# Sparse attention feeding an MLP mixer: the global sums moved into the next period, three transposes put into PV's PSUM slot, scores spaced by two dense tiles

## The chip, the cores and the metric

The kernel runs on one core of a Trainium2 chip. Its engines are named here as the profile names them: PE (TensorE, matrix products), DVE (VectorE), ACT (ScalarE), POOL (GpSimd) and SP (SyncE, which only issues transfers). The metric is the device time of one execution in microseconds, as the median of repeated runs.

## The reference

The kernel computes a sparse attention followed by a token and channel mixer.

```python
# q, k, v: [8, 8, 576, 64] (batch, head, token, dim); 8 global tokens
scores = q @ k.T / sqrt(64)
mask = |i - j| <= 32  or  i is global  or  j is global
x = softmax(scores where mask else -1e9) @ v      # -> [8, 576, 512], heads side by side
h = relu(x.T @ w_tok1) @ w_tok2                   # tokens 576 -> 256 -> 576
u = x + h.T
out = u + relu(u @ w_ch1) @ w_ch2                 # channels 512 -> 1536 -> 512
```

The inputs and the output are float32; the kernel computes in float16 and sums in float32.

## The kernel before

**Batches and tiles.** The eight batches go through the kernel one behind the other. The 576 tokens of a batch are four tiles of 128 and one of 64. Heads go in four pairs, p = 0 to 3. The last 64 tokens of two batches share one tile in the channel mixer, which is therefore done in the odd batches.

**The steps of a batch**, with their functions (lines in the listing below and in the profile):

- casts (L383, L386): the loaded q and k go to float16, mostly on ACT. `casts(b)` is a list of ten, c(0) to c(4) are its pairs: the last 64 tokens, then head pairs 0 to 3.
- `TR` (L427) transposes the last 64 tokens on PE; `TRE` (L438) copies the result out on DVE.
- `T(b, p)` (L400) transposes q and k of a head pair on PE, eight 128x128 transposes into one PSUM tile pT; `TE` copies it out on DVE, q at L406 and k at L412. `t` is both.
- `globals_` (L392) puts the global tokens' queries beside the others.
- `S_(b, p, part)` (L458): banded scores, in two parts, each followed by its exponential on ACT (L470). `s2` is both parts. `SM` (L476 `eg`, L481 `e_all`) masks them on DVE and picks out `eg`, the weights of the global rows.
- `GK` (L515 to L517): scores of the global keys; exponential on ACT (L527, L528), mask on DVE (L532).
- `v_odd` (L373, L374): a copy of v shifted by 64 tokens, two DVE copies.
- `OG` (L539): the global rows' sums over all tokens, twenty small matmuls that read `eg` of all four head pairs; DVE spreads the result into `rf` (L544).
- `PV(b, tau)` (L656, L665): the attention's output for one token tile, from `rf`, the masked exponentials and v. DVE divides by the row sums (L678, L679) and writes x.
- `M1(b, ch)` (L692): token mixer in, one token tile at a time; after the last one ACT takes the ReLU (L700; in batch 1 ACT and DVE take half each, L697 and L698) and writes `a1`.
- `M2(b, part)` (L716): token mixer out, in three parts; DVE adds x and writes `u` (L721, the last part L724). `M3` (L733, L736) turns u into `uT` with transposing DMAs on SP's queue; in batch 1 `M3p` does it on PE (L745, L747).
- `M4(b, j)` (L755): channel mixer in, twelve tiles of four 128x512 matmuls, each followed by a ReLU on ACT (L758). `M4l` is the same for the shared last tile.
- `M5(b, tau, part)` (L781): channel mixer out, two parts of six 128x512 matmuls for each token tile; DVE adds u (L785, the last tile L788) and writes `osb`, which SP stores.

M4, M4l and M5 are the *dense tiles*. All the rest is the sparse work.

**Periods.** Period b interleaves the dense tiles of batch b with the sparse work of later batches: `n = b + 1` is finished (PV, M1, M2, M3), and `m = b + 2` is begun (T, S, GK). The order is written out by hand. In the lists below `D` (None) stands for "the next dense tile"; `play` takes the list from left to right, and puts dense tiles that are left over at its end. Period 0 has its own list (`period_0`). Period 1 is merged by weights (`sparse2`, `merge`); in it T(3,1) and T(3,2) come out next to each other. Periods 2 to 7 play `first_half` with the twelve M4 (and three M4l in odd periods) and `second_half` with the eight or ten M5. Period 6 has nothing of batch m, and period 7 is dense tiles alone. Batch 0's sparse work is done ahead of period 0, in another order.

Every engine works its instructions in the order in which the lists emit them. So a step's place in a list sets its place in the queues of PE, DVE, ACT and SP alike.

**PSUM.** Three pools share the eight banks. psS (`pss`) has two slots of two banks, psV (`psv`) one slot of two banks, psM (`psm`) two slots of one bank. The slots of a pool are used in turn, and a tile waits until the slot's last tile has been read. psM holds the results of M4, M4l and M5 (and T and TR of batches 0 and 2). psS holds S, M1, M2 and the odd PV. psV holds GK, OG and the even PV, in batches other than 2. T and TR take a slot by the expressions in their first lines, which the change edits. In the kernel before, T(m, p) of batches from 3 on lies in psS for even p and in psV for odd p.

**Loads.** SP loads q and k of the batch after next once the casts of the batch before have read the buffers, ahead of the transposing DMAs of M3 in its queue. POOL loads v once PV has read the old one.

Of the kernel before, what the change touches and what calls it, by code (L numbers as in the profile page):

```python
# [9 lines left out]
F16 = mybir.dt.float16  # L10
# [5 lines left out]
P = 128  # L16
NT = 5
# [27 lines left out]
def kernel(  # L45
# [13 lines left out]
    B, H, S, D = q.shape  # L59
# [4 lines left out]
    NP = H // 2  # L64
# [306 lines left out]
    def v_odd(b, hs=slice(0, H), eng=nc.vector):  # L371
        i = b % 2
        eng.tensor_copy(out=vod[i][HQ:P, :, hs], in_=vsh[i][HQ:P, 0 : NT - 1, hs])  # L373
        eng.tensor_copy(out=vod[i][0:HQ, :, hs], in_=vsh[i][0:HQ, 1:NT, hs])  # L374
# [16 lines left out]
    def globals_(b):  # L391
        nc.vector.tensor_copy(  # L392
            out=qTs[b % 2][:, :, :, 0:NG], in_=gT[:, b].unsqueeze(2).to_broadcast([P, NP, NT, NG])
        )

    def T(b, p):
        pT = (psm if b in (0, 2) else psv if b == 1 or p % 2 else pss)([P, 2, 512], F16, name=f"pT_{b}_{p}")
        for ti, n in enumerate((qn, kn)):
            for i in range(4):
                nc.tensor.transpose(  # L400
                    out=pT[:, ti, P * i : P * i + P], in_=n[b % 2][:, i, 2 * p : 2 * p + 2, :], identity=ident
                )
        st[b]["pT", p] = pT
# [15 lines left out]
        TEk(b, p)  # L419

    def TR(b):
        pr = (psm if b in (0, 2) else psv)([P, 2, 4, NP * 16], name=f"pr_{b}")
        sel = ident.rearrange("p (n r x) -> p r n x", n=NP, r=2)
        for ti, n in enumerate((qr, kr)):
            for i in range(4):
                for par in range(2):
                    nc.tensor.matmul(  # L427
                        pr[64 * par : 64 * par + 64, ti, i, :], lhsT=n[b % 2][:, i, :], rhs=sel[:, par], start=True, stop=True
                    )
        st[b]["pr"] = pr  # L430
        if b > 0:
            TRE(b)
# [39 lines left out]
    def SM(b, p):  # L472
        e2 = e_all[:, 2 * p : 2 * p + 2]
        if b > 0:
            gc = bass.AP(tensor=e2.tensor, offset=e2.offset, ap=[e2.ap[0], [QS, NT], [ES, 2], [1, NG]])
            nc.vector.tensor_tensor(  # L476
                out=eg[:, :, 2 * p : 2 * p + 2, 0:NG], in0=gc, in1=egm.unsqueeze(2).to_broadcast([P, NT, 2, NG]), op=ALU.mult
            )
        bm = bandm.rearrange("p c x -> p (c x)")[:, 0:ES]
        for par in range(2):  # L480
            nc.vector.tensor_mul(out=e2[:, par], in0=e2[:, par], in1=bm)  # L481
# [26 lines left out]
    def GK(b):  # L508
        s = st[b]
        ps = (psv if b != 2 else pss)([P, 2, 512], name=f"gk_{b}")  # L510
        for p in range(NP):
            o = ps[32 * p : 32 * p + 32]
            qv = qTs[b % 2][:, p, :, NG:QS]
            w = kgz[:, b, p, :]
            nc.tensor.matmul(o[:, 0, 0:384], lhsT=w, rhs=qv[:, 0:3], start=True, stop=True)  # L515
            nc.tensor.matmul(o[:, 1, 0:128], lhsT=w, rhs=qv[:, 3], start=True, stop=True)
            nc.tensor.matmul(o[:, 1, 128:192], lhsT=w, rhs=qv[:, 4, 0:LAST], start=True, stop=True)  # L517
        s["gk"] = ps
        if b > 0:
            LX(b)  # L520
            LM(b)
# [8 lines left out]
    def LM(b):  # L530
        lf = st[b]["lf"]
        nc.vector.tensor_mul(out=lf, in0=lf, in1=mf)  # L532

    def OG(b):
        s = st[b]
        ps = (psv if b != 2 else pss)([P, 2, VW], name=f"og_{b}")
        for c in range(NT):
            for p in range(NP):
                nc.tensor.matmul(  # L539
                    ps[32 * p : 32 * p + 32], lhsT=eg[:, c, 2 * p : 2 * p + 2, :],  # L540
                    rhs=vsh[b % 2][:, c, 2 * p : 2 * p + 2, :], start=(c == 0), stop=(c == NT - 1),
                )
        rf = mb.tile([P, NP, 2, VW], F16, tag="rf", name=f"rf_{b}")
        nc.vector.tensor_tensor(  # L544
            out=rf, in0=ps.unsqueeze(1).to_broadcast([P, NP, 2, VW]),
            in1=blk.rearrange("p (n r) -> p n r", r=2).unsqueeze(3).to_broadcast([P, NP, 2, VW]), op=ALU.mult,
        )
        s["rf"] = rf
# [135 lines left out]
    def M1(b, ch):  # L684
        s = st[b]
        if ch == 0:
            ps = pss([P, 2, 512], name=f"a1p_{b}")
            s["a1p"], s["a1pp"] = [ps[:, 0], ps[:, 1]], ps
        ps = s["a1p"]
        for tt in range(2):  # L690
            w = w1[:, ch, P * tt : P * tt + P] if ch < NT - 1 else w1l[:, b % 2, P * tt : P * tt + P]
            nc.tensor.matmul(ps[tt], lhsT=w, rhs=x16s[b % 2][:, ch, :], start=(ch == 0), stop=(ch == NT - 1))  # L692
        if ch < NT - 1:
            return
        a1 = mb.tile([P, 2, DM], F16, tag="a1", bufs=1, name=f"a1_{b}")
        if b == 1:
            nc.scalar.activation(out=a1[:, 0], in_=s["a1pp"][:, 0], func=AF.Relu)  # L697
            nc.vector.tensor_scalar(out=a1[:, 1], in0=s["a1pp"][:, 1], scalar1=0.0, scalar2=None, op0=ALU.max)  # L698
        else:
            nc.scalar.activation(out=a1, in_=s["a1pp"], func=AF.Relu)  # L700
        s["a1"] = a1
        s["u16"] = mb.tile([P, 4, DM], F16, tag="u16", name=f"u16_{b}")
        if b % 2 == 0:
            s["ul"] = mb.tile([P, DM], F16, tag="ul", name=f"ul_{b}")
        else:
            s["ul"] = st[b - 1]["ul"]
# [85 lines left out]
    def t(b, p):  # L792
        T(b, p)
        TE(b, p)
# [37 lines left out]
    def s2(b, p):  # L832
        return lambda: (S_(b, p, 0), S_(b, p, 1))

    def period_0():
        n, m = 1, 2
        D = None
        c2 = casts(m)
        c1 = [lambda ti=ti, p=p: cast_qk(1, ti, p, nc.scalar.copy) for p in (2, 3) for ti in range(2)]
        u = [D, D, D, D, D, D, lambda: TR(n), lambda: globals_(n), D, lambda: t(n, 0), *c1[:2], D]  # L840
        u += [lambda: t(n, 1), *c1[2:], lambda: (load_qk1(2), load_v16(2)), D, s2(n, 0), D, lambda: t(n, 2), lambda: SM(n, 0), D, s2(n, 1), D]
        u += [lambda: t(n, 3), lambda: SM(n, 1), s2(n, 2), lambda: v_odd(n), D, lambda: SM(n, 2), lambda: GK(n), s2(n, 3), D]
        u += [lambda: SM(n, 3), lambda: OG(n), D, lambda: PV(n, 0), lambda: PV(n, 1), D, lambda: PV(n, 2), lambda: PV(n, 3), D]
        u += [*c2, lambda: PV(n, 4), lambda: [M1(n, ch) for ch in range(NT - 1)], D, lambda: M1(n, NT - 1), lambda: globals_(m), D]
        u += [lambda: M2(n, 0), lambda: M2(n, 1), lambda: TR(m), D, lambda: M3p(n, 0), lambda: t(m, 0)]
        u += [lambda: M3p(n, 1), lambda: (M2(n, 2), M3(n, 2)), lambda: t(m, 1)]
        u += [s2(m, 0), lambda: t(m, 2), lambda: SM(m, 0)]
        return u

        return u  # L850

    def first_half(b):
        n, m = b + 1, b + 2
        D = None
        cs = casts(m) if m < B else []

        def c(k):
            return cs[2 * k : 2 * k + 2]

        def tt(p):  # L860
            return [lambda: t(m, p)] if m < B else []

        def pv(tau):
            return lambda: PV(n, tau)

        if n == B:
            return []
        u = [D, *([lambda: OG(n)] if b == 2 else []), D, pv(0), pv(1), *c(0), D, *c(1), D, pv(2), pv(3), *c(2), D, lambda: [M1(n, ch) for ch in range(3)], D]
        if b == 2:
            u += [lambda: gather_t(1)]  # L870
        u += [pv(4), *c(3), D, lambda: M1(n, 3), D, *([lambda: TR(m)] if m < B else []), lambda: M1(n, 4), *c(4)]
        if m < B:
            u += [lambda: load_v16(m), lambda: globals_(m)]
        if m + 1 < B:
            u += [lambda: (load_rest(m + 1), load_qk(m + 1, slice(0, H)))]
        u += [D, *tt(0), D, lambda: (M2(n, 0), M3(n, 0)), D, *tt(1), lambda: (M2(n, 1), M3(n, 1)), D, *tt(2)]
        u += [lambda: (M2(n, 2), M3(n, 2) if n % 2 else None), D]
        return u

    def second_half(b):  # L880
        m = b + 2
        D = None
        if m >= B:
            return []
        return [D, s2(m, 0), D, lambda: t(m, 3), lambda: SM(m, 0), D, s2(m, 1), D, lambda: SM(m, 1), D, s2(m, 2), D,
                lambda: SM(m, 2), lambda: GK(m), lambda: v_odd(m), s2(m, 3), D, lambda: SM(m, 3), D, lambda: OG(m)]

    def dense(b):
        u = [(0.86, lambda j=j: M4(b, j)) for j in range(NJ)]
# [188 lines left out]
```

## Time and profile before

| | |
|---|---|
| median of 14 runs | 335.9 us (333.7 to 339.18) |
| profiled execution | 339.65 us, of which the profile's span is 337.6 us |
| PE busy | 317.0 us, 94% of the span |
| DVE, ACT, POOL busy | 192.2, 155.4, 62.2 us |
| M4 and M5 on PE (L755, L781) | 94.9 and 102.3 us busy |
| mean granted PE clock | 0.977 |
| period 2 / 3 / 4 / 5 / 6 begins (its first M4) | 128.39 / 164.93 / 204.54 / 238.71 / 278.31 us |

The span runs from the first to the last instruction; the execution's own time has some 2 us around it. A PE instruction's shown length includes the time until its result has left the array, while the next one starts before that; therefore the distance from start to start tells what a group of matmuls costs. A row of the timeline has start, length, engine, line, operation, output and inputs, shape, count, and in brackets the idle time before it with what ended it. A row of a windows answer gives for a stretch of time the busy time of PE, PE's weight loads, DVE, ACT and POOL, then the granted PE clock as a share of full speed, and the DMA load. In the page's second part the granted PE clock stands in tenths for 40 equal slices of the span.

### The profile page before, as it was taken

The page shows a single profiled execution, that of the slowest core. Times are in us where ns is not written, and L with a number is a line of the kernel's source. Part 1 is how long each engine was busy: PE and PEld are TensorE (multiplying, and loading weights), DVE is VectorE, ACT ScalarE, POOL GpSimd, SP SyncE. Part 2 cuts the span into 40 slices and gives each one's busy share as a digit, 9 for nine tenths or more (in the row PEclk, how much of TensorE's full clock was granted, in tenths as well). Part 3 has the DMA queues.
Part 4 walks back from the last instruction along what each step waited for, and adds up shares of the span by engine and source line. Part 5 has one row for each costly group of instructions (what it writes and reads, how often), then busy time and mean ns, then how long its engine had stood idle before and what let it go on. Part 6 is the DMA issues. An engine that isn't in the chain of part 4 may idle for free.

```text
span 337.6 us, 8236 instructions
## 1 busy us (share of the span) xinstructions
PE 317.0 (94%) x3505; PEld 175.8 (52%) x3505; DVE 192.2 (57%) x414; ACT 155.4 (46%) x281; POOL 62.2 (18%) x95
## 2 busy tenths in 40 slices
PE   4988999798899999999999999999999999999994
PEld 4757845355446544454455645444556445444641
DVE  7385557658952777485737475477737564231021
ACT  3460378702848045654475444744474333503600
POOL 5696569130021001300030002200000000000000
PEclk9996799799999999999999999999999999999998
DMA  7999997991877952969196714995102121051013
GB/s 207 210 145 222 279 182 225 172 111 54 202 124 76 264 163 58 90 207 184 65 93 192 161 65 90 75 265 133 58 0 49 49 94 33 2 140 62 2 63 92
DMA packets 78198, 41.85 MB, mean 124 GB/s; under 512 B 54482, under 2 KB 72274, under 8 KB 78162
## 3 DMA queue, kind: packets, MB, share of 16 engines
q0 software_dynamic: 38608, 12.88, 31.6%
q1 hardware_dynamic: 39552, 28.45, 31.5%
q8 instruction: 27, 0.44, 0.6%
q14 instruction: 9, 0.07, 0.1%
q10 hardware_dynamic: 2, 0.00, 0.0%
HBM read 36.11 MB, written 9.44 MB: 135 GB/s over the span
## 4 chain that ended last, share of the span: by engine, by line
PE 78%; DVE 16%; issue 3%; ACT 2%; DVEq 0%; ACTq 0%
PE op L781 24%; PE b1p L755 21%; PE a1p L692 5%; PE hp L716 4%; PE pv L656 3%; PE b1lp L768 3%; PE pT L400 3%; PE pv L665 3%; PE s L458 3%; DVE e_all L481 2%; DVE kT L412 2%; DVE vod L373 1%; DVE vod L374 1%; DVE qT L406 1%; PE warm L208 1%
## 5 line engine op out<-in xcount | busy, mean ns | idle before, releaser
L755 PE MATMUL b1p<-uT,wc 128*128 128x512 f16 x384 | 94.9, 380 | 0.8 <-ACT b L758 0.6
L758 ACT ACTIVATE b<-b1p 128x512 f16<-128x512 f32 x96 | 57.0, 598 | 76.8 <-PE b1p L755 76.8
L781 PE MATMUL op<-wc,b 128*128 128x512 f16 x384 | 91.1, 383 | 0.0
L470 ACT ACTIVATE e_all<-s 128x544 f16<-128x544 f32 (+1 forms) x64 | 40.9, 685 | 38.4 <-issue 26.0
L781 PEld LDWEIGHTS <-b 128*128 128x128 f16 x384 | 35.4, 98 | 39.5 <-issue 0.8
L755 PEld LDWEIGHTS <-wc 128*128 128x128 f16 x384 | 35.0, 98 | 39.8 <-issue 2.2
L361 POOL DMA_DIRECT2D vsh<-in_v_dram x35 | 29.5, 849 | 140.5 <-DVE rr L678 125.6
L785 DVE TENSOR_TENSOR osb<-u,op 128x512 f32<-128x512 f16 x32 | 22.0, 686 | 53.2 <-PE op L781 51.0
L678 DVE RECIPROCAL rr<-pv 128x8 f32<-128x8 f32 (+1 forms) x35 | 7.1, 204 | 32.4 <-PE pv L665 32.4
L481 DVE TENSOR_TENSOR e_all<-e_all,bandm 128x616 f16<-128x616 f16 x56 | 24.3, 476 | 1.0
L679 DVE TENSOR_TENSOR x<-pv,rr 128x512 f16<-128x512 f32 (+1 forms) x35 | 24.2, 691 | 1.2
L406 DVE COPY qT<-pT 128x512 f16<-128x512 f16 x30 | 20.6, 686 | 7.2 <-PE pT L400 6.8
L721 DVE TENSOR_TENSOR u<-x,hp 128x1024 f16<-128x1024 f16 x14 | 17.0, 1218 | 12.1 <-PE hp L716 12.1
L412 DVE COPY kT<-pT 128x512 f16<-128x512 f16 x30 | 20.4, 682 | 1.9 <-PE pT L400 1.3
L716 PE MATMUL hp<-a,w 128*128 128x512 f16 x72 | 19.1, 379 | 1.3 <-DVE u L721 1.3
L656 PE MATMUL pv<-rf,lf 128*64 128x264 f16 x126 | 18.7, 288 | 0.9 <-DVE kgz L355 0.7
L665 PEld LDWEIGHTS <-e_all 128*64 128x64 f16 x504 | 18.3, 112 | 0.2
L665 PE MATMUL pv<-vsh,e_all 128*64 128x66 f16 x280 | 18.4, 196 | 0.0
L386 ACT CAST qn<-lq 128x512 f16<-128x512 f32 x27 | 16.6, 614 | 3.5 <-DMA lq<-in_q_dram 3.5
L386 ACT CAST kn<-lk 128x512 f16<-128x512 f32 x27 | 16.8, 621 | 1.5 <-DMA lk<-in_k_dram 1.5
L458 PE MATMUL s<-qT,kT 64*64 64x136 f16 (+2 forms) x704 | 16.3, 216 | 1.2 <-DVE ul L724 0.7
L458 PEld LDWEIGHTS <-kT 64*64 64x64 f16 x704 | 10.8, 107 | 12.6 <-issue 10.9
(175 smaller groups left out, 366.1 us busy)
## 6 DMA issues: line engine op xcount, KB each, us to landing
out_dram<-osb SPq DMA_DIRECT2D x32, 256.0 KB
lq<-in_q_dram SPq DMA_DIRECT2D x5, 1024.0 KB
lk<-in_k_dram SPq DMA_DIRECT2D x5, 1024.0 KB
wc<-in_moe_w_ch_dram POOLq DMA_DIRECT2D x6, 512.0 KB
vsh<-in_v_dram POOLq DMA_DIRECT2D x21, 128.0 KB
lq<-in_q_dram POOLq DMA_DIRECT2D x2, 1024.0 KB
lk<-in_k_dram POOLq DMA_DIRECT2D x2, 1024.0 KB
vsh<-in_v_dram POOLq DMA_DIRECT2D x14, 96.0 KB
```

The costliest lines, as they stand in the source:

```text
L361: nc.gpsimd.dma_start(out=vsh[b % 2][r0:r1, c, :, 0:D], in_=v[b, :, j0 : j0 + (r1 - r0), :].rearrange("h p d -> p h d"),)
L386: eng(out=(qn, kn)[ti][b % 2][:, :, hs].rearrange("p i h d -> p h i d"), in_=(lq, lk)[ti][:, hs])
L412: eng(out=kTs[b % 2][:, p, WIN : WIN + 512].rearrange("p (x i) -> p x i", i=4), in_=st[b]["pT", p][:, 1].rearrange("p (i x) -> p x i", i=4),)
L458: nc.tensor.matmul(ps[o, par, i0 - a : i1 - a], lhsT=kT[r, HQ * j : HQ * j + HQ], rhs=qf[r, i0:i1], start=b > 0, stop=b > 0 or j in js[-2:],)
L470: nc.scalar.activation(out=e2[:, :, a:z], in_=ps[:, :, 0 : z - a], func=AF.Exp, scale=scale)
L481: nc.vector.tensor_mul(out=e2[:, par], in0=e2[:, par], in1=bm)
L656: nc.tensor.matmul(ps[r0 : r0 + 64, hf, 0 : NP * VW], lhsT=s["lf"][:, HQ * t : HQ * t + HQ], rhs=s["rf"][:, 2 * hf : 2 * hf + 2], start=Tr ...
L665: nc.tensor.matmul(ps[r0 : r0 + 64, hf, VW * hh : VW * hh + VW], lhsT=e_all[:, h, lo : lo + HQ], rhs=(vod if t % 2 else vsh)[b % 2][:, tau ...
L716: nc.tensor.matmul(ps[:, i, :], lhsT=w2[:, ch, P * tau - sh : P * tau - sh + P], rhs=s["a1"][:, ch, :], start=(ch == 0), stop=(ch == 1),)
L755: nc.tensor.matmul(ps, lhsT=wc1[:, cc, P * j : P * j + P], rhs=s["uT"][:, cc, :], start=(cc == 0), stop=(cc == 3))
L758: nc.scalar.activation(out=s["b1"][:, j, :], in_=ps, func=AF.Relu)
L781: nc.tensor.matmul(ps, lhsT=w, rhs=wc2[:, j, :], start=(j == 0), stop=(j == NJ - 1))
```

## The change

Nothing is added or removed; slots and orders change.

- T(m, p) of batches from 3 on: p = 1, 2 and 3 all take psV; only p = 0 takes psS. TR of batch 1 takes psS instead of psV.
- Period 0: v_odd stands behind S(1,3) and a dense tile; OG stands one dense tile later; the dense tile between M1(1,4) and M2(1,0) is gone from there (it is the one ahead of OG).
- Periods 2 to 6, `first_half`: OG(n) stands behind the period's first dense tile and ahead of two more, then PV. Before, it stood at the end of the last period (in period 2, as now, behind the first dense tile). The casts c(0) to c(4) come earlier. No dense tile is left between M1(n,4) and T(m,0). T(m,2) stands behind M2's second part and a dense tile, and T(m,3) behind M2's third part, where before it was in the second half.
- Periods 2 to 5, `second_half`: T(m,3) and OG(m) are gone. S(m,1) stands two dense tiles behind S(m,0), S(m,2) two behind S(m,1); v_odd comes one dense tile earlier.

```diff
     def T(b, p):
-        pT = (psm if b in (0, 2) else psv if b == 1 or p % 2 else pss)([P, 2, 512], F16, name=f"pT_{b}_{p}")
+        pT = (psm if b in (0, 2) else psv if b == 1 or p > 0 else pss)([P, 2, 512], F16, name=f"pT_{b}_{p}")
     def TR(b):
-        pr = (psm if b in (0, 2) else psv)([P, 2, 4, NP * 16], name=f"pr_{b}")
+        pr = (psm if b in (0, 2) else pss if b == 1 else psv)([P, 2, 4, NP * 16], name=f"pr_{b}")
     def period_0():
-        u += [lambda: t(n, 3), lambda: SM(n, 1), s2(n, 2), lambda: v_odd(n), D, lambda: SM(n, 2), lambda: GK(n), s2(n, 3), D]
-        u += [lambda: SM(n, 3), lambda: OG(n), D, lambda: PV(n, 0), lambda: PV(n, 1), D, lambda: PV(n, 2), lambda: PV(n, 3), D]
-        u += [*c2, lambda: PV(n, 4), lambda: [M1(n, ch) for ch in range(NT - 1)], D, lambda: M1(n, NT - 1), lambda: globals_(m), D]
+        u += [lambda: t(n, 3), lambda: SM(n, 1), s2(n, 2), D, lambda: SM(n, 2), lambda: GK(n), s2(n, 3), D]
+        u += [lambda: v_odd(n), lambda: SM(n, 3), D, lambda: OG(n), D, lambda: PV(n, 0), lambda: PV(n, 1), D, lambda: PV(n, 2), lambda: PV(n, 3), D]
+        u += [*c2, lambda: PV(n, 4), lambda: [M1(n, ch) for ch in range(NT - 1)], D, lambda: M1(n, NT - 1), lambda: globals_(m)]
         u += [lambda: M2(n, 0), lambda: M2(n, 1), lambda: TR(m), D, lambda: M3p(n, 0), lambda: t(m, 0)]
     def first_half(b):
-        u = [D, *([lambda: OG(n)] if b == 2 else []), D, pv(0), pv(1), *c(0), D, *c(1), D, pv(2), pv(3), *c(2), D, lambda: [M1(n, ch) for ch in range(3)], D]
+        u = [D, lambda: OG(n), *c(0), D, D, pv(0), pv(1), *c(1), D, *c(2), D, pv(2), pv(3), D, lambda: [M1(n, ch) for ch in range(3)], *c(3), D]
         if b == 2:
             u += [lambda: gather_t(1)]
-        u += [pv(4), *c(3), D, lambda: M1(n, 3), D, *([lambda: TR(m)] if m < B else []), lambda: M1(n, 4), *c(4)]
+        u += [pv(4), D, lambda: M1(n, 3), *c(4), D, *([lambda: TR(m)] if m < B else []), lambda: M1(n, 4)]
         ...
-        u += [D, *tt(0), D, lambda: (M2(n, 0), M3(n, 0)), D, *tt(1), lambda: (M2(n, 1), M3(n, 1)), D, *tt(2)]
-        u += [lambda: (M2(n, 2), M3(n, 2) if n % 2 else None), D]
+        u += [*tt(0), D, lambda: (M2(n, 0), M3(n, 0)), *tt(1), D, lambda: (M2(n, 1), M3(n, 1)), *tt(2), D]
+        u += [lambda: (M2(n, 2), M3(n, 2) if n % 2 else None), *tt(3)]
     def second_half(b):
-        return [D, s2(m, 0), D, lambda: t(m, 3), lambda: SM(m, 0), D, s2(m, 1), D, lambda: SM(m, 1), D, s2(m, 2), D,
-                lambda: SM(m, 2), lambda: GK(m), lambda: v_odd(m), s2(m, 3), D, lambda: SM(m, 3), D, lambda: OG(m)]
+        return [D, s2(m, 0), D, D, lambda: SM(m, 0), s2(m, 1), D, lambda: SM(m, 1), D, s2(m, 2), lambda: v_odd(m), D, lambda: SM(m, 2),
+                lambda: GK(m), s2(m, 3), D, lambda: SM(m, 3), D]
```

## The prediction

> **What bounds the kernel now.** I read the shares and the clock row, then the chain of work, then TensorE's and VectorE's timelines of one period at a time.
>
> ```profile
> PE 317.0 (94%) x3505; PEld 175.8 (52%) x3505; DVE 192.2 (57%) x414; ACT 155.4 (46%) x281; POOL 62.2 (18%) x95
> ...
> PEclk9996799799999999999999999999999999999998
> ...
> PE 78%; DVE 16%; issue 3%; ACT 2%; DVEq 0%; ACTq 0%
> ```
>
> TensorE is busy nearly throughout and owns the chain; VectorE's 16% are the places where TensorE stands still for it. The change adds no work, so I only ask where these stops are, which go and which come. TensorE, period 3:
>
> ```profile
> 183.01 1.03 PE L755 MATMUL b1p<-uT,wc 128*128 128x512 f16 x4
> 183.87 0.39 PE L400 MATMUL pT<-ident,qn 128*128 128x128 f16 x4
> 184.09 0.39 PE L400 MATMUL pT<-ident,kn 128*128 128x128 f16 x4
> 184.81 0.59 PE L716 MATMUL hp<-a,w 128*128 128x512 f16 x2 [0.33 <-DVE u L721]
> ...
> 201.20 0.80 PE L539 MATMUL og<-vsh,eg 128*32 128x132 f16 x20
> ```
>
> From start to start an unhindered T takes 0.45 us (181.70 to 182.14); this one takes 0.94: 0.49 lost, since M2 waits for a psS slot. OG runs from 201.20 to the next start at 201.94, 0.74; unhindered it needs 0.42 (62.02 to 62.41 for its last seventeen matmuls): 0.32 lost to `eg`. At the end of even periods the first two M4 take 2.06 (164.93 to 166.99) instead of 1.83: 0.23 lost to an `osb` that frees a psM slot. VectorE beside it:
>
> ```profile
> 182.34 0.69 DVE L406 COPY qT<-pT 128x512 f16<-128x512 f16 x1
> 182.95 0.68 DVE L412 COPY kT<-pT 128x512 f16<-128x512 f16 x1
> 183.55 1.21 DVE L721 TENSOR_TENSOR u<-x,hp 128x1024 f16<-128x1024 f16 x1
> 184.68 0.68 DVE L406 COPY qT<-pT 128x512 f16<-128x512 f16 x1
> ```
>
> So a pair of TE copies holds VectorE 1.20 us, one `u` 1.13; a copy's result is there 0.68 after its start, and TensorE goes on 0.06 later (`u` ends at 184.76, M2 starts at 184.81). A copy starts 0.20 after its matmuls' end. Period 1, TensorE, then VectorE:
>
> ```profile
> 116.61 0.39 PE L400 MATMUL pT<-ident,qn 128*128 128x128 f16 x4
> ...
> 117.06 0.39 PE L400 MATMUL pT<-ident,qn 128*128 128x128 f16 x4
> ...
> 117.51 1.46 PE L781 MATMUL op<-wc,b 128*128 128x512 f16 x6
> 118.86 0.38 PE L400 MATMUL pT<-ident,qn 128*128 128x128 f16 x4
> ```
>
> ```profile
> 116.84 0.68 DVE L785 TENSOR_TENSOR osb<-u,op 128x512 f32<-128x512 f16 x1
> 117.43 0.68 DVE L406 COPY qT<-pT 128x512 f16<-128x512 f16 x1
> 118.03 0.68 DVE L412 COPY kT<-pT 128x512 f16<-128x512 f16 x1
> ```
>
> T(3,1) and T(3,2) run back to back because they lie in different slots; the first is evacuated only at 118.71. Last, period 0's OG, and the windows over what follows it:
>
> ```profile
> 59.97 0.30 PE L539 MATMUL og<-vsh,eg 128*32 128x132 f16 x3
> 62.02 0.46 PE L539 MATMUL og<-vsh,eg 128*32 128x132 f16 x17 [1.75 <-DVE eg L476]
> 62.41 2.58 PE L781 MATMUL op<-wc,b 128*128 128x512 f16 x6
> ```
>
> ```profile
> 62.60:66.00 3.40, 3.40 (x28) 1.59 (x28) 0.89 (x2) 3.20 (x7) 0.00 (x0) 0.50 1.83 163
> ```
>
> OG stands 2.0 us, and then the clock is at half rate for 3.4 us: six M5 take 2.51 and PV 1.58 where they take 1.40 and 1.08 elsewhere, 1.6 us more.
>
> **What the Trainium skill says.** "PSUM — Partial Sum Buffer", PSUM bank collisions raise a hardware error, has every reuse of a bank guarded by a semaphore: a one-slot pool makes each new T wait for the last one's evacuation; the 0.49 above is such a wait. "TensorE: Matmul & The Clock Gate", Part 1, says ScalarE and VectorE are strict FIFO and matmuls keep program order, so a T that waits holds up all behind it; the trace agrees (M2 at 184.81 waits in place). The same part gives a free-running activity window of 3413 ns after which a lightly used array falls to half rate; the trace shows one such stretch from 62.6 to 66.0 after the 2.0 us stop. As the window is free-running, that loss need not come in every execution.
>
> **The change part by part**, t = 0 at M1(n,4)'s end, in us.
>
> *First half, periods 2 to 5.* Now M1, T0, dense, M2(0), T1, dense, M2(1), T2, dense, M2(2), T3. `a1` (L700, 1.02) starts 0.26 after M1 (143.47 to 143.73), so M2(0) may go at 1.34; T0 (0.45) and a dense tile (0.86) reach 1.31: 0.03 to 0.10 lost, I take 0.07 (the casts c(4) now stand ahead of it on ScalarE, two of 0.50, but end about 0.6 before M1 does; without that cover up to 1.0). M2(0) 1.38 to 2.24; `u` 2.44 to 3.57. T1 at 2.24 finds psV free. Dense, M2(1) to 4.42. T2 would start at 4.42, but TE(1) waits behind `u`: 3.57 to 4.77, result at 4.17+0.68 = 4.85; T2 at 4.91, **0.49 lost**. The next `u` 4.77 to 5.90. T2, dense, M2(2) end at 6.65; TE(2) 5.90 to 7.10, result at 7.18; T3 at 7.24, **0.59 lost**. Old stop here 0.49. Net +0.66 a period, four periods: **+2.6**.
>
> *Period 1* changes only through T's slots: T(3,2) goes from psS to psV. T2 may start at 118.77 instead of 117.06: 1.71 lost; TE(2) runs 119.41 to 120.6, result at 120.69; T3 follows the M5 at 120.5 and waits to 120.75. T3 was at 118.86: **+1.9**. Nothing after it has slack of its own: exponentials, `eg` and OG all hang on TensorE.
>
> *Second half.* T3 is gone from it. SM and v_odd keep their order; v_odd's two copies (0.73 each) go ahead of the third `osb`. `eg`(3) is written 1.7 us before OG, which stands behind one more M4; the last `osb` frees its slot 0.5 before the second M4. Without these covers the old 0.32 and 0.23 come back. Gain 0.32 at the ends of periods 2 to 5, 0.23 at 2 and 4: **-1.7**. Period 2's PV no longer waits for `rf` (M4 1.13 instead of 0.97): **-0.2**.
>
> *Period 6* has no T between M1(7,4) and M2(7,0): one dense tile (0.86) against `a1` ready at 1.34 (290.54 to 290.80, + 1.02 + 0.06): **+0.5**.
>
> *Period 0.* TR(1) in psS spares T(1,0) the wait for TR's copies: -0.28. S(1,3) then ends at 58.29, two dense tiles at 60.98, and OG starts. VectorE: `osb` 59.79 to 60.40 (its M5 ends at 59.59), v_odd to 61.86, `eg` to 62.05: OG stops for 1.05 instead of 2.0 and ends at 62.48. From there to M1(1,4)'s end, at full clock, 1.40 + 1.08 + 1.40 + 1.08 + 1.40 + 0.60 + 1.74 + 1.30 + 0.43 = 10.43 in both orders (M5, PV, M5, PV, M5, PV, M1, M5, M1): 72.91 now, 72.84 before with its OG ending at 62.41. But the dense tile put ahead of OG is missing behind M1(1,4), where it covered `a1` (74.70 to 76.03); TensorE now stands about 1.5 there, and M2(1,0) ends as long after M1(1,4) as before (2.3). So the tile moved from one stop to another: **0.0**. The stop of 1.05 leaves two thirds of a window busy, so the half-rate stretch should go: **-1.6 where it was**. T(1,p) and T(2,p) keep their slots.
>
> *Queues.* SP's loads of the next q and k wait for c(4) and are issued some 2 us earlier, ahead of the transposing DMAs as before; `uT` is due 15 us after its `u`. POOL's loads of v wait for PV, 0.9 later, and are read 30 us on. Both are hidden; a late `uT` would stop M4 by its full lateness.
>
> Sum: 2.6 + 1.9 - 1.7 - 0.2 + 0.5 = +3.1. The profiled execution (339.65, span 337.6, 2.05 around it) had the half-rate stretch: 339.65 + 3.1 - 1.6 = 341.1. It lies 3.75 above the median 335.9 and at the top of the runs shown (333.7 to 339.18), which stand in three groups about 2 us apart, as if such stretches came in some and not in others. So for the median I count half of the 1.6: 335.9 + 3.1 - 0.8 = **338.2**.
>
> **The rivals.** *The clock pays in full* (18%): the median run had the stretch; 335.9 + 3.1 - 1.6 = 337.4. For: 59.2 to 62.6 is idle by more than half. Against: the lower half of the runs. *A new half-rate stretch* (15%): period 1's stop of 1.7 leaves about half of a window busy; the stop at 60 us left less than half. 338.2 + 1.6 = 339.8. *Half the waits* (12%): TE comes sooner than its queue lets me think, all nine new waits are half as long, -3.1: 335.1. *Faster* (5%): T2 and T3 find psV free, because the copies do not queue behind `u` and `osb`; 1.9 + 4 x 1.08 = 6.2 less, 332.0. It decides for faster once the nine waits sum to under 2.2. Against: thirty copies of 0.68 with hardly a spread, in a fixed order. That the edits do nothing is excluded, as the slots and orders differ in every period.
>
> **How the numbers follow.** Forecast 50%, its own range 337.2 to 339.2. 0.5% (1.7 us: below 334.2, above 337.6) is about what can be told from no change. Above 337.6 lie nine tenths of the forecast, the new stretch and a little of the full clock gain: 0.64; faster 0.05; the rest 0.31. The range 336.4 to 340.3 leaves out the two fast cases and the tail of the slow one; the unknown wake-up (0.06 to 0.13 in nine places) moves it by 0.6 at most.
>
> **What would show it.** TensorE: in periods 2 to 5 a stop of about 0.5 before T2 and 0.6 before T3, released by L412; one of 1.7 before T(3,2) in period 1; OG without a stop from period 3 on; about 1.05 before OG and 1.5 in M2 in period 0; 0.5 before M2(7,0). In the clock row no half rate near 62 us. Wrong if the T stops are missing, if half rate shows near 118 us, or if period 0's end moves by more than the clock.

## The result and the profile after

The changed kernel takes 339.8 us (median of 10 runs, 337.97 to 341.27); beside it the kernel before took 334.76 us (47 runs). The ratio is 1.0139, 95% interval 1.0109 to 1.0169: about 4.7 us slower. The forecast was 338.2 us in a range of 336.4 to 340.3, slower.

Executions of one kernel differ by several us with their mean granted PE clock; "at full clock" below means the median over the executions whose mean clock was 0.995 or more. At full clock the kernel before takes 334.5 us (53 of the 106 executions that ran beside the experiments below) and the changed one 338.25 (6 of 12): +3.8 us. The other half of the changed kernel's executions lies at clocks of 0.984 to 0.991, mostly near 340.7, which is why its median over all is higher.

The page of the profiled execution after (337.49 us, span 335.4): busy shares, clock row, and the chain's shares.

```profile
PE 309.4 (92%) x3505; PEld 168.7 (50%) x3505; DVE 193.5 (58%) x414; ACT 156.6 (47%) x281; POOL 62.8 (19%) x95
...
PEclk9999999999999999999999999999999999999998
...
PE 77%; DVE 16%; issue 3%; ACT 3%; DVEq 0%; ACTq 0%
```

The work is the same and PE's busy time is 7.6 us lower, yet the kernel is slower. The profile of before had two stretches of half rate, the one from 62.6 to 66.0 us that the prediction shows and a longer one ahead of period 0; this one has none before its last 2 us. A windows row of the longer one, before:

```profile
28.50:38.70 10.20, 10.20 (x132) 9.15 (x130) 4.72 (x9) 1.54 (x4) 5.45 (x10) 0.50 1.11 291
```

At half rate the same matmuls are busy for longer, so the two spans can't be compared as they stand. The periods can, since both ran periods 1 to 7 at full rate (first M4 to first M4, us):

| period | 0 | 1 | 2 | 3 | 4 | 5 | 6 | 7 |
|---|---|---|---|---|---|---|---|---|
| before | 44.10 (1.6 of it half rate) | 43.10 | 36.54 | 39.61 | 34.17 | 39.60 | 28.20 | 31.09 |
| after | 43.74 | 45.11 | 36.17 | 39.65 | 34.38 | 39.64 | 29.09 | 31.10 |

Periods 1 to 7 sum to +2.8. What is left of the 3.8, about 1.0, must come from period 0 or from ahead of it; more on its size below. PE's timeline of period 3, after (start, length, engine, line, operation, tiles, shape, count, idle time before it and its releaser):

```profile
178.99 1.03 PE L716 MATMUL hp<-a,w 128*128 128x512 f16 x4
180.36 0.40 PE L400 MATMUL pT<-ident,qn 128*128 128x128 f16 x4 [0.34 <-DVE kT L412]
180.59 0.39 PE L400 MATMUL pT<-ident,kn 128*128 128x128 f16 x4
180.82 1.03 PE L755 MATMUL b1p<-uT,wc 128*128 128x512 f16 x4
181.68 0.59 PE L716 MATMUL hp<-a,w 128*128 128x512 f16 x2
182.69 0.40 PE L400 MATMUL pT<-ident,qn 128*128 128x128 f16 x4 [0.41 <-DVE kT L412]
```

M2's second part takes 1.37 from start to start instead of 0.86 (178.99 to 180.36): T(5,2) stands 0.51. M2's third part takes 1.01 instead of 0.43: T(5,3) stands 0.58. DVE beside it:

```profile
180.22 1.21 DVE L721 TENSOR_TENSOR u<-x,hp 128x1024 f16<-128x1024 f16 x1
181.35 0.68 DVE L406 COPY qT<-pT 128x512 f16<-128x512 f16 x1
181.95 0.68 DVE L412 COPY kT<-pT 128x512 f16<-128x512 f16 x1
```

The copy that ends at 182.63 lets T go 0.06 later. In period 1 the one slot costs most:

```profile
111.78 0.39 PE L400 MATMUL pT<-ident,kn 128*128 128x128 f16 x4
113.72 0.40 PE L400 MATMUL pT<-ident,qn 128*128 128x128 f16 x4 [1.55 <-DVE kT L412]
...
114.17 1.46 PE L781 MATMUL op<-wc,b 128*128 128x512 f16 x6
115.81 0.38 PE L400 MATMUL pT<-ident,qn 128*128 128x128 f16 x4 [0.18 <-DVE kT L412]
```

T(3,1) starts at 111.56, T(3,2) 2.16 later instead of 0.45 (1.7 lost), and T(3,3) starts 1.64 after the M5 ahead of it instead of 1.35 (0.3 more). Period 0 after, up to OG:

```profile
51.02 0.31 PE L458 MATMUL s<-qT,kT 64*64 64x72 f16 x10
52.02 0.34 PE L458 MATMUL s<-qT,kT 64*64 64x72 f16 x12 [0.69 <-ACT e_all L470]
...
57.17 0.24 PE L539 MATMUL og<-vsh,eg 128*32 128x132 f16 x3
58.55 0.46 PE L539 MATMUL og<-vsh,eg 128*32 128x132 f16 x17 [1.15 <-DVE eg L476]
```

OG stands 1.38 (start to start, three matmuls of which are work), and S(1,2)'s second part stands 0.89, which it did not in the profile of before.

### The profile page after: what moved, and what is told of

Its sections match the earlier page's. It is cut to its first block, busy times and chain, and to the rows that moved or that the text cites. A ratio compares the mean times of both kernels' runs of the same rounds, so it can differ in the third digit from the quotient of the medians.

```text
span 335.4 us, 8238 instructions
## 1 busy us (share of the span) xinstructions
PE 309.4 (92%) x3505; PEld 168.7 (50%) x3505; DVE 193.5 (58%) x414; ACT 156.6 (47%) x281; POOL 62.8 (19%) x95
## 4 chain that ended last, share of the span: by engine, by line
PE 77%; DVE 16%; issue 3%; ACT 3%; DVEq 0%; ACTq 0%
PE op L781 27%; PE b1p L755 21%; PE a1p L692 5%; PE s L458 3%; PE pv L656 3%; PE b1lp L768 3%; PE hp L716 3%; DVE kT L412 3%; DVE qT L406 3%; PE pv L665 3%; PE pT L400 3%; DVE u L721 2%; DVE vod L373 1%; PE og L539 1%; DVE vod L374 1%
## 5 line engine op out<-in xcount | busy, mean ns | idle before, releaser
L781 PE MATMUL op<-wc,b 128*128 128x512 f16 x384 | 89.2, 380 | 0.0
L412 DVE COPY kT<-pT 128x512 f16<-128x512 f16 x30 | 20.4, 682 | 1.4 <-PE pT L400 0.9
L400 PE MATMUL pT<-ident,qn 128*128 128x128 f16 x128 | 13.0, 226 | 5.5 <-DVE kT L412 5.4
```

Of the source, the lines that this page charges most:

```text
L412: eng(out=kTs[b % 2][:, p, WIN : WIN + 512].rearrange("p (x i) -> p x i", i=4), in_=st[b]["pT", p][:, 1].rearrange("p (i x) -> p x i", i=4),)
L781: nc.tensor.matmul(ps, lhsT=w, rhs=wc2[:, j, :], start=(j == 0), stop=(j == NJ - 1))
```

## The experiments

My theory: psV's one slot is the loss (period 1 and four times T2 and T3), and the moves of OG, SM and v_odd gain a little. Rivals: VectorE's queue is the bound and would make PE wait whatever the slot; the granted clock makes the difference; period 0's order does.

### The kernel before once more

No edit.

> The kernel before, unchanged, for the clock rows of further executions. If the loss is TensorE's stops alone, its time from period 0's first M4 to the end is about 294.8 us at full clock (296.4 in the first profile less the 1.6 of its half-rate stretch), against 298.9 in the kernel after. If the loss is mostly the clock, few of its executions have a mean clock under 0.99, where about half of those of the kernel after do (0.984 to 0.987, 340.2 to 341.3 us, against 0.991 to 0.997, 337.5 to 338.6 us).

335.38 us (14 runs, 333.37 to 338.96), ratio 0.997 (0.9927 to 1.0014); 334.25 at full clock. Its profile again fell on an execution with the two half-rate stretches:

```profile
PEclk9996799799999999999999999999999999999998
```

Its period 0 takes 44.09, as in the first profile, and OG in it 2.44, of which it stands 2.0. Half of this kernel's executions have a mean clock of 0.995 or more, so the median execution has hardly any half rate: the 1.6 us that the stretch behind OG costs belongs to the profiled execution, not to the median. The longer stretch ahead of period 0 costs that execution more: period 0 begins at 41.19 in the first profile and at 40.49 in this one, and at 35.39 to 37.83 in the ten traces without it, some 4 us earlier. The rival that the granted clock makes the difference falls: low clocks came no more often with the change, 40 of 106 executions under 0.99 without it and 5 of 12 with it.

### T's slots back in turn

```diff
-        pT = (psm if b in (0, 2) else psv if b == 1 or p > 0 else pss)(...)
+        pT = (psm if b in (0, 2) else psv if b == 1 or p % 2 else pss)(...)
```

> The kernel after with T's slots as before the change (p odd in psV, p even in psS), order unchanged. Theory of the stops: T(3,2) no longer waits (-2.1 with its tail), and in periods 2 to 5 T2 waits for nothing, M2's third part 0.3 for its u, T3 for nothing: 0.37 a period with a1's 0.07 instead of 1.15, so -3.1. Together 5.2 below the kernel after: 332.8 us against its 338.0 at full clock, and about 1 to 2 us below the kernel before. Theory of the clock: it stays within 1 us of the kernel after, 337 to 341. Theory that VectorE's queue and not the slots is what T3 waits for: only the stop moves, to M2's third part and to S, and no more than 2.1 comes back.

333.12 us (22 runs), ratio 0.9963 (0.9934 to 0.9992): with its slots back, the changed kernel beats the kernel before. At full clock 333.0, 5.25 below the changed kernel. Period 1 takes 43.10, periods 2 to 5 take 35.39, 38.86, 33.59 and 38.86, which is 0.78 or 0.79 less in each. Period 3, PE:

```profile
176.88 1.03 PE L716 MATMUL hp<-a,w 128*128 128x512 f16 x4
177.74 0.39 PE L400 MATMUL pT<-ident,qn 128*128 128x128 f16 x4
...
178.19 1.03 PE L755 MATMUL b1p<-uT,wc 128*128 128x512 f16 x4
179.37 0.59 PE L716 MATMUL hp<-a,w 128*128 128x512 f16 x2 [0.15 <-DVE u L721]
179.80 0.39 PE L400 MATMUL pT<-ident,qn 128*128 128x128 f16 x4
```

T2 and T3 (177.74, 179.80) start as soon as the matmuls before them have gone. What comes in their place is M2's third part, which waits for a psS slot: 1.18 from 178.19 to 179.37 where the dense tile takes 0.86, so 0.32. The stops of 0.51 and 0.58 were the slot, less these 0.32; the order of VectorE's queue is the same here, so the rival that this queue makes PE wait whatever the slot falls.

### Only T(3,2) back in psS

```diff
+        pT = (... psv if b == 1 or (p > 0 and (b, p) != (3, 2)) else pss)(...)
```

> The kernel after with T(3,2) alone back in psS. Theory of the stops: period 1 (first M4 to first M4) goes from 45.1 back to 43.1 us, all else as after: 2.1 below the kernel after at equal clock, about 335.9. Theory of the clock: under 0.5 of difference beyond the share of half-rate executions.

336.9 us (22 runs), ratio 1.0046 (1.0015 to 1.0077); 336.15 at full clock, 2.1 below the changed kernel. Period 1 takes 43.09; periods 2 to 7 are those of the changed kernel within 0.01 to 0.02.

```profile
112.82 0.39 PE L400 MATMUL pT<-ident,kn 128*128 128x128 f16 x4
113.05 0.39 PE L400 MATMUL pT<-ident,qn 128*128 128x128 f16 x4
113.27 0.39 PE L400 MATMUL pT<-ident,kn 128*128 128x128 f16 x4
```

The two T run back to back again. One tile's slot in one period is worth 2.0 us; the slots of T2 in periods 2 to 5 are worth the other 3.1.

### T3 alone back in psS

```diff
+        pT = (psm if b in (0, 2) else psv if b == 1 or p in (1, 2) else pss)(...)
```

> The changed kernel with T(m,3) alone back in psS (T(m,1) and T(m,2) in psV). It tells whether T2's and T3's stops are two costs or one: Theory (each wait for psV's one slot costs by itself): T3's stop of 0.58 us is gone in periods 2 to 5 and T2's 0.51 stays; the periods are 0.58 shorter each less up to 0.3 that a wait for a psS slot may give back in the next M2 or S; period 1 gains 0.3 of its own 2.0 at most. In all -1.5 to -2.6 against the changed kernel: 337.2 to 338.3 us. Rival (VectorE's queue is the bound there, and whatever comes next waits as long): the periods stay within 0.1 us of the changed kernel's, 339 to 340 us.

337.5 us (6 runs), ratio 1.0106 (1.0043 to 1.0169); 336.84 at full clock, 1.4 below the changed kernel. Periods 3 and 5 take 39.06, 0.58 less than the changed kernel's; periods 2 and 4 take 36.26 and 34.44, no less than its 36.17 and 34.38. So the answer is different in even and odd periods. Period 2, PE:

```profile
147.55 0.39 PE L400 MATMUL pT<-ident,qn 128*128 128x128 f16 x4
147.77 0.39 PE L400 MATMUL pT<-ident,kn 128*128 128x128 f16 x4
148.00 1.46 PE L781 MATMUL op<-wc,b 128*128 128x512 f16 x6
149.38 0.31 PE L458 MATMUL s<-qT,kT 64*64 64x72 f16 x10
150.16 0.34 PE L458 MATMUL s<-qT,kT 64*64 64x72 f16 x12 [0.47 <-DVE kT L412]
```

T3 starts at once, but then S(m,0)'s second part stands 0.66 for psS, until VectorE has copied T3 out of it. In odd periods three M4l (2.68 us) lie between T3 and S and hide that copy. Neither theory nor rival was right throughout: T3's stop is a cost of its own only where something covers its evacuation.

### Period 0's old order

```diff
-        u += [lambda: t(n, 3), lambda: SM(n, 1), s2(n, 2), D, ...]
-        u += [lambda: v_odd(n), lambda: SM(n, 3), D, lambda: OG(n), ...]
-        u += [..., lambda: globals_(m)]
+        u += [lambda: t(n, 3), lambda: SM(n, 1), s2(n, 2), lambda: v_odd(n), D, ...]
+        u += [lambda: SM(n, 3), lambda: OG(n), ...]
+        u += [..., lambda: globals_(m), D]
```

> The kernel after with period 0's order as before the change, slots kept. Theory of the stops: at full clock as the kernel after, within 0.4 us; OG stops for 2.0 us again, M2(1,0) hardly at all. If the 0.9 us before S(1,2)'s second part and the longer OG stop in the profile after belong to the new order, it is 1.2 below the kernel after. The half-rate stretch near 60 us is back in some of the executions, 1.6 us each; none has it without the 2.0 us stop.

339.08 us (6 runs), ratio 1.012 (1.0047 to 1.0192). Only one of the six was at full clock (337.13, the profiled one), so its time says little. Its period 0 takes 43.25 against 43.74, and OG in it stands 1.66, not the 2.0 expected. The pair of the slots alone and the combined kernel below tells more.

### OG's move alone, on the kernel before

```diff
-        u = [D, *([lambda: OG(n)] if b == 2 else []), D, pv(0), pv(1), ...]
+        u = [D, lambda: OG(n), D, D, pv(0), pv(1), ...]
-        u += [D, *tt(0), D, lambda: (M2(n, 0), M3(n, 0)), ...]
+        u += [*tt(0), D, lambda: (M2(n, 0), M3(n, 0)), ...]
-        ... lambda: SM(m, 3), D, lambda: OG(m)]
+        ... lambda: SM(m, 3), D]
```

> The kernel before with only the global sums' move: OG(n) one dense tile after the period's head, two dense tiles behind it up to PV, and for these the dense tile between M1(n,4) and T(m,0) gone; T's slots, the place of T(m,3), SM, v_odd and period 0 stay as before. Theory (the move is worth what the prediction's terms say): OG runs without its 0.32 us stop at the ends of periods 2 to 5 (-1.3), the first M4s after it lose their 0.23 (-0.5), a1 adds 0.07 in four periods (+0.3) and 0.47 in period 6: about -1.0, so 334.1 us beside 335.1. Rival (the stop only moves to the next instruction that needs what VectorE does, PV or M4): 335.1 to 335.6, with PV or M4 standing some 0.3 us in each period.

334.01 us (22 runs), ratio 0.9966 (0.9936 to 0.9995). The median is the 334.1 of the theory, but with help of the clock: only 3 of its 22 executions lie under 0.99. At full clock it takes 333.8, 0.4 less than the kernel before in the same set (334.2). By its trace too the gain is smaller than the terms: periods 1 to 7 sum to 251.83 against 252.31, -0.5 where -1.0 was expected. The head of period 3, PE, then DVE:

```profile
158.69 0.47 PE L539 MATMUL og<-vsh,eg 128*32 128x132 f16 x20
159.67 1.89 PE L755 MATMUL b1p<-uT,wc 128*128 128x512 f16 x8 [0.51 <-DVE osb L785]
```

```profile
156.56 0.71 DVE L373 COPY vod<-vsh 64x2112 f16<-64x2112 f16 x1
157.30 0.70 DVE L374 COPY vod<-vsh 64x2112 f16<-64x2112 f16 x1
157.93 0.19 DVE L476 TENSOR_TENSOR eg<-e_all,egm 128x80 f16<-128x80 f16 x1
158.15 0.87 DVE L481 TENSOR_TENSOR e_all<-e_all,bandm 128x616 f16<-128x616 f16 x2
158.94 0.68 DVE L785 TENSOR_TENSOR osb<-u,op 128x512 f32<-128x512 f16 x1
```

OG no longer stands (0.98 to the next start, of which 0.40 is its own), but the M4 behind it does, 0.57: the last `osb` is queued behind v_odd and SM and frees its psM slot late. In the slots-back and in the changed kernel, where v_odd comes a dense tile earlier, this stop isn't there. So OG's move alone doesn't bring the second half's gain. That v_odd's earlier place is what covers the `osb`, as the prediction had it, fits these lines; it was not tried alone, and SM and T(m,3) move in those kernels as well. Period 0 has the old order here: at full rate it takes 43.66.

### Slots and period 0 back, a tile more in period 6

On top of the slots in turn and period 0's old order:

```diff
-        u += [*tt(0), D, lambda: (M2(n, 0), M3(n, 0)), ...]
+        u += [*tt(0), *([] if m < B else [D]), D, lambda: (M2(n, 0), M3(n, 0)), ...]
```

> The changed kernel with three things undone or mended: T's slots back to psV and psS in turn, period 0's old order back, and in period 6, where no T stands between M1(7,4) and M2(7,0), a second dense tile there. By the traces so far: with the slots alone 333.1 us; period 0's old order ran 0.9 us shorter than the new at the same clock when the stop before S(1,2)'s second part is left out; period 6 loses its 0.47. Theory (the three are independent): 333.1 - 0.9 - 0.5 = 331.7 us. Rival (period 0's gain is taken back by the stop before S(1,2), which was 1.3 there and 0.8 with the slots alone): 332.4 us or more.

331.91 us (21 runs), ratio 0.9918 (0.9887 to 0.9949); 331.5 at full clock, 1.5 below the slots alone. Period 6 takes 28.64 instead of 29.10 (-0.46: the stop of M2(7,0) is gone), which leaves 1.0 for period 0's old order. The two kernels ran in different sets, though, whose kernel before took 334.6 and 334.2 at full clock; each set against its own, 0.6 is left. The profiled execution shows next to nothing of it: period 0 takes 43.82 (43.88 with the slots alone), with this in it:

```profile
51.63 0.31 PE L458 MATMUL s<-qT,kT 64*64 64x72 f16 x10
53.16 0.34 PE L458 MATMUL s<-qT,kT 64*64 64x72 f16 x12 [1.22 <-ACT e_all L470]
```

S(1,2)'s second part stands 1.41 here, T(1,1) 0.6 more than usual.

### The gathers of k behind the loads

```diff
-    gather(1)
+    gather(1, (0,))
-        u += [..., lambda: (load_qk1(2), load_v16(2)), D, s2(n, 0), ...]
+        u += [..., lambda: (load_qk1(2), load_v16(2), gather(1, (1,))), D, s2(n, 0), ...]
```

> As the run before it, but the two indirect gathers of k for the second half of the batches, which GpSimd issues some 13 us after period 0's head, stand behind the loads of the next q, k and v in its queue, some 4 us later (their rows are used in period 2). In every trace so far ScalarE and VectorE took up TensorE's work 0.7 to 1.2 us late once in period 0, just while the last of these gathers was issued. Theory (the gather's issue holds up TensorE's signals): no stop before S(1,2)'s second part, -0.8 to -1.2 in period 0, and either no late signal or one some 4 us on that meets no wait; 0.5 to 1 us less than the run before it. Rival (something else at that place, such as TensorE's instruction fetch at the same time): the stop of 0.7 to 1.2 stays before S(1,2)'s second part and the times are equal within 0.3 us.

331.58 us (19 runs), ratio 0.9891 (0.9859 to 0.9924); 331.2 at full clock, 0.3 below the run before it. ScalarE's timeline of the changed kernel, then of this one:

```profile
49.81 0.62 ACT L470 ACTIVATE e_all<-s 128x544 f16<-128x544 f32 x1
51.23 0.74 ACT L470 ACTIVATE e_all<-s 128x688 f16<-128x688 f32 x1 [0.80 <-PE pT L400]
```

```profile
51.15 1.26 ACT L470 ACTIVATE e_all<-s 128x544 f16<-128x544 f32 x2
```

The two exponentials of S(1,1) run back to back and S(1,2) doesn't stand. PE's instruction fetch is still there (50.5 to 51.7 us in this trace), so it is not enough by itself. But what is saved there comes back: OG, reached earlier, stands 1.98 instead of 1.66, and then the clock falls. This trace, windows (PE, its loads, DVE, ACT and POOL busy, granted clock, DMA load):

```profile
58.00:62.00 4.00, 3.38 (x39) 1.57 (x41) 2.06 (x5) 0.71 (x2) 2.02 (x2) 0.69 1.90 210
```

That is the pattern of the profile before: no stop at S(1,2), 2.0 at OG, then half rate.

### v_odd in period 0 back at its old place

The slots in turn, and in the new order of period 0:

```diff
-        u += [..., s2(n, 2), D, lambda: SM(n, 2), lambda: GK(n), s2(n, 3), D]
-        u += [lambda: v_odd(n), lambda: SM(n, 3), D, lambda: OG(n), ...]
+        u += [..., s2(n, 2), lambda: v_odd(n), D, lambda: SM(n, 2), lambda: GK(n), s2(n, 3), D]
+        u += [lambda: SM(n, 3), D, lambda: OG(n), ...]
```

> The changed kernel with T's slots back to psV and psS in turn, and with v_odd(1) in period 0 back at its old place ahead of SM(1,2); the dense tile ahead of OG stays there and none stands behind M1(1,4). It tells why OG, a dense tile later in period 0, still stood 1.4 to 1.6 us where 1.05 was forecast. Theory (VectorE idles 0.8 us between lf and osb because v_odd is queued behind that osb, and v_odd's two copies then stand whole between osb and the last eg): VectorE does v_odd while it waited, the idle time goes, OG's stop falls by 0.7 to 0.8, to about 0.8, and the time by as much: 332.4 us beside the 333.1 of the slots alone. Rival (the last eg is late because of ScalarE's exponential or the held-up signals, not because of v_odd): OG's stop stays at 1.4 to 1.6 and the time at 333.1.

332.53 us (6 runs), ratio 0.9894 (0.9833 to 0.9955); 331.5 at full clock (4 executions; the kernel before beside it 333.7). DVE in the changed kernel, then here:

```profile
54.98 0.46 DVE L532 TENSOR_TENSOR lf<-lf,mf 128x576 f16<-128x576 f16 x1 [0.23 <-ACT lf L528]
55.98 0.69 DVE L785 TENSOR_TENSOR osb<-u,op 128x512 f32<-128x512 f16 x1 [0.55 <-PE op L781]
56.70 0.71 DVE L373 COPY vod<-vsh 64x2112 f16<-64x2112 f16 x1
57.44 0.96 DVE L374 COPY vod<-vsh 64x2112 f16<-64x2112 f16 x1
58.32 0.18 DVE L476 TENSOR_TENSOR eg<-e_all,egm 128x80 f16<-128x80 f16 x1
```

```profile
56.06 0.45 DVE L532 TENSOR_TENSOR lf<-lf,mf 128x576 f16<-128x576 f16 x1
56.43 0.68 DVE L785 TENSOR_TENSOR osb<-u,op 128x512 f32<-128x512 f16 x1
57.02 0.19 DVE L476 TENSOR_TENSOR eg<-e_all,egm 128x80 f16<-128x80 f16 x1
```

In the changed kernel VectorE idles 0.23 and 0.55 while v_odd, which needs nothing new, stands behind an `osb` that waits for PE; then v_odd's 1.6 us lie between that `osb` and the `eg` OG needs. Here the idle time is gone and OG stands 0.75 (56.51 to 57.27 in PE's timeline), as expected. The profiled execution has half rate later on (71.15 to 74.56) and a period 0 of 44.93: M2 stands 1.63 for `a1` there, for ACT's ReLU of M1 (69.25) is queued behind casts that had waited for the load of k until 65.61.

### The same, with period 6's tile and the gathers moved

The run before with period 6's second tile and with the gathers of k behind the loads.

> The run before it with period 6's second dense tile between M1(7,4) and M2(7,0) and with the gathers of k behind the loads. Against the combined kernel with the gathers moved (331.6) it keeps the dense tile ahead of OG instead of behind M1(1,4). Theory (OG's stop becomes short, about 1.0 where 2.0 was, so that no half-rate stretch follows, while M1 and M2 stand 1.3 more for a1): 331.6 - 1.0 + 1.3 - 1.3 (the tile itself, spent earlier) = 330.6 us where the stretch is avoided, without a half-rate stretch after OG. Rival (the two orders of period 0 differ only in where TensorE stands): 331.6 within 0.3.

331.43 us (21 runs), ratio 0.9917 (0.9887 to 0.9946). It shows no half rate, OG stands 0.89, and its period 0 takes 42.48, the shortest of all; still, at full clock it takes 331.2, like the run with the old order and the gathers moved. The rival holds: the old and the new order of period 0, each at its best, differ in where PE stands, not in the sum. The slots alone beat the kernel before by 0.4%, the four versions from the combined one on by 0.8 to 1.1%; the runs don't rank these four.

## Why the prediction was right, and where it was off

The time lies in the range and the direction is right, and periods 1 to 7 took the path foreseen. The size of the change was not right: +2.3 was forecast (338.2 from 335.9), and +4.7 came by the ratio. That the time still lies in the range is in part luck: the median of 14 runs it started from, 335.9, lay 1.1 above the 334.76 of the 47 beside the result. The parts that were off are period 0 and the clock.

**First half, +2.6.** Right. T2 stops for 0.51 (0.49 foreseen), T3 for 0.58 (0.59), `a1` costs 0.03 in period 2 and nothing in 3 to 5 (0.07), and L412 releases both T. The old stop of 0.49 is gone: +0.6 a period, +2.4. That these are the slot's doing, and not the queue's alone, is shown by the slots put back; a T in the other pool leaves 0.32 of it in M2, and in even periods T3 alone in the other pool only moves its stop to S.

**Period 1, +1.9.** Right: +2.0, and the one slot given back takes it away.

**Second half, -1.7, and period 2's PV, -0.2.** Right together, as far as the periods tell: with the first half and period 6, periods 2 to 7 should come to +1.2 and came to +0.8. OG's own stop is gone from period 3 on. OG moved alone showed that a cover is needed (0.57 in M4); that it is v_odd's place is argued from VectorE's lines.

**Period 6, +0.5.** Right: 0.47, and one more dense tile removes 0.46.

**Period 0, 0.0.** This step failed; it was between +0.3 and +1.0. Its second part held: from OG's end to the period's end, every trace at full rate takes 21.27 or 21.28, in the old order and the new. Behind OG the new order thus has one dense tile less and stands as much more: M1's last part takes 1.35 instead of 0.43, and M2's eight matmuls 2.32 instead of the 1.94 of the old order. What failed is "OG stops for 1.05 instead of 2.0". It stands 1.38 to 1.64 in four traces of the new order, because v_odd got behind an `osb` that VectorE waits for; and in three traces of the old order at full clock it stands not 2.0 but 1.59 to 1.66. The 2.0 came from an execution that had not stood at S(1,2) before. So the tile ahead of OG buys 0.1 on average instead of 0.95, while its absence behind M1(1,4) costs all it was foreseen to. How much the period loses by this, the runs don't settle. Four traces of the changed order at full rate have a period 0 of 43.86 on average (43.60 to 44.21) and three of the old one 43.58 (43.25 to 43.82): +0.3, since the old order stands longer at T(1,1) and S(1,2). The timed pair, 333.0 and 331.5 less period 6's 0.46, says 1.0, or 0.6 with each set against its own kernel before.

**The clock, -1.6 where it was, half of it for the median.** The half-rate stretch did go from the profiled execution. For the median it was counted wrongly: half of the executions before, and so about the median one, had no such stretch. Nor was it the larger one: the sum is silent on the half rate ahead of period 0, some 4 us, which is most of what the profiled 339.65 had over the median. Without the -0.8 the sum at full clock is 334.5 + 2.8 and 0.3 to 1.0 for period 0, so 337.6 to 338.3, where 338.25 was measured. The median of 339.8 lies between two groups of the ten timed runs, five of which ran at 0.984 to 0.987 and took 340.2 to 341.3; where in the kernel they lost it, no trace shows. That the median fell between the groups is chance.

**The rivals.** A new half-rate stretch at period 1's stop did not come in the profile: the clock row is full there after 1.7 us of standing. The profile is of an execution at full clock, so it can't speak for the five at low clock, and the rival's number, 339.8, is the one measured. What speaks against it is that low clocks were as frequent without that stop: 8 of 22 executions lie under 0.99 with T(3,2) alone back, and 8 of 22 with all slots back. Half the waits: excluded, the nine waits came at 98 to 106% of the size foreseen. Faster, with T2 and T3 finding psV free: excluded by L412 as releaser.

## What to carry to other kernels

A tile moved into a one-slot pool costs the wait for its predecessor's evacuation, counted through the queue of the engine that evacuates, and here the sum came out of one profile to 0.1 us a stop. Before moving filler work ahead of a wait, look at what ends the wait: where the engine that ends it idles or gets other work put in between, the filler buys nothing there and is missing where it was. And a stop seen in a disturbed execution is not the stop of the typical one; compare stages of several executions before pricing it.

## What the hardware showed unexpectedly

**PE's signals late.** In seven of the ten traces with the gathers in place, ScalarE and VectorE took up PE's work late once in period 0. In the changed kernel S(1,1)'s second part ends at 49.67 and no signal of PE is recorded from then to 51.21, though PE goes on to issue at its usual pace; the exponential that waits for it starts at 51.23. POOL issues the last of four indirect gathers from 49.64 to 50.58, and PE's instruction fetch runs from 49.5 to 50.5. In the profile of before and in its repeat nothing starts late: there the gather is over (at 50.86 and 50.02) before the fetch begins (at 51.3 and 51.0). With the gathers moved the fetch is alone at this place, and nothing starts late there, in two traces. So the two at the same time fit eleven of the twelve traces; but in the twelfth (v_odd's) both fall together and nothing is late. The gathers' part is likely and not shown, and the mechanism stays open.

**Half rate after a half-empty window.** In all twelve traces the granted clock changes only at whole multiples of 3.41 us from its other changes. Cut into windows of this grid, PE was busy for 0.49 of the window ahead of the half-rate stretch behind OG in the profile of before and in its repeat, 0.46 with the gathers moved, and 0.42 ahead of the stretch at 71.15 in v_odd's trace. No other window from period 0's first M4 to 320 us, in any trace, is under 0.55, and none of the others was followed by half rate: not period 1's stop in the changed kernel (111.55 to 114.96, 0.55), nor OG's in it (56.94 to 60.35, 0.66). OG's stop of 1.98 us and period 1's of 1.7 thus lie on different sides of a limit between 0.49 and 0.55. That limit is an estimate from these windows, and not the whole rule: the stretch ahead of period 0 came after windows with 0.73 and 0.81, and one at a kernel's very end (OG moved alone, 0.48) was not followed by half rate at once.
